# A convolution and low-rank mixer on one core: turning U first, mixing group 0 from parts, a third x buffer, group 2 mixed a round earlier

## The chip, the core and the metric

The kernel runs on one core of a Trainium2 chip. The core has a matrix engine (TensorE, PE in the profile; PEld is its weight load), VectorE (DVE), ScalarE (ACT), GpSimd (POOL) and SyncE (SP, which here only issues transfers), and sixteen DMA engines that all queues share. PE writes to PSUM; DVE and ACT carry results from PSUM to SBUF. The metric is the device time of one execution in microseconds, lower is better; the time quoted for a kernel is the median of its runs.

## The reference

All inputs are float32: `x` (8, 4224, 192), `weight` (8, 7), `U` (4224, 32), `V` (32, 4224), `w_ch1` (192, 768), `w_ch2` (768, 192).

```python
w = softmax(weight)                                  # per head, over 7 taps
out = einsum('hk,bskhg->bshg', w, x_unf)             # causal convolution along the sequence, 8 heads of 24 channels
x = out.reshape(B, S, D)
xt = x.transpose(0, 2, 1)
h = xt @ U @ V                                       # mixes along the sequence, rank 32
u = x + h.transpose(0, 2, 1)
ch = np.maximum(u @ w_ch1, 0.0) @ w_ch2
return (u + ch).astype(np.float32)
```

## The kernel before, in words

A sequence of 4224 positions is 33 tiles of 128 rows, so the eight batches have 264 tiles. Instructions are issued in an order written out by hand; each engine runs its own in that order and waits on semaphores.

*Per batch.* `load_x` (L87) brings x from HBM on POOL's queue and casts it to bfloat16. The convolution (`conv_two`, L355 to L377) is a product of x with a banded 128 x 128 matrix per head (`band_sb`), two heads at a time; DVE and ACT evict it to `y_sb`. In batches 0 and 1 a second band matrix takes in the rows of the tile before; later batches get these rows from `conv_halo` and `put_halo`. `low_rank` (L414) multiplies the 33 tiles with U and adds them up in four parts, one for each 32 partitions; `fold` (L434) adds the four with one float32 product against `fold_sb`, and gives `tt_sb`, which lies twice, in partitions 0 to 31 and 64 to 95.

*Per group of 8 tiles* (33 groups). `mix_quad` (L443) multiplies V with `tt_sb` for four tiles, and two DVE additions (L467) add `y_sb` and write `u_sb`. `u_sb` must then be turned to channels by rows: group 1 by PE (`turn`, L526 and L537), all later ones by a transposing DMA on SP's queue (`turn_by_dma`, L542); group 0 is made in turned form at once by `straight` (y turned by PE, L488) and `straight_mix` (V mixed onto it in the same PSUM bank, L504, evicted at L513 and L515). `h1_chunk` (L560) forms six chunks with W1, each evicted with a relu by ACT (L570; chunks 0, 2, 4, 5) or DVE (L572; chunks 1, 3). `w2_step` (L582) multiplies with W2; after 24 of its 48 steps per group DVE adds u (L593), and SP stores the result (L600).

*Rounds.* Round g runs `h1_chunk` for group g, then the second half of the W2 steps of group g-1 and the first half of group g's, in eight pieces. Beside the pieces stand other steps, by a table (`beside`): the turn and the mixing of group g+2, and the convolution, low rank and fold of batches to come. A step with place END comes after the last piece. In rounds 0 to 2:

- round 0: h1 of group 0; quads of group 1 and 0; W2 steps; the PE turn of group 1
- round 1: a quad of group 2, h1 of group 1, the other quad of group 2; the turn of group 2 by DMA after piece 2; the convolution of batch 1; at the end its low rank, and between its steps the two quads of group 3 and the turn of group 3 by DMA
- round 2: a quad of group 4, h1 of group 2, the other quad; `build_halo_band` (L315) at piece 0

*Start.* U arrives with 33 rows of 4096 numbers and is turned by PE in four lots of eight float32 transposes (`turn_U`, L192), evicted by `evict_U`; two lots come ahead of batch 0's convolution, two inside it. x of batch 0 comes in five loads (`blocks_0`). `load_others` brings V, W1, W2 and batch 1.

*Pools that matter.* All PSUM is one pool of four two-bank tiles (`big`), taken in rotation by every step: a tile is free when its last user has been evicted. `xs`, the x buffers, has two; the loads of batch 2 and later wait for the convolution of the batch two before.

Of the kernel before, what the change touches and what calls it, by code (L numbers as in the profile page):

```python
# [15 lines left out]
def kernel(  # L16
# [39 lines left out]
    dram = ctx.enter_context(tc.tile_pool(name="dram", bufs=2, space=bass.MemoryType.DRAM))  # L56
    xs = ctx.enter_context(tc.tile_pool(name="xs", bufs=2))
    hxs = ctx.enter_context(tc.tile_pool(name="hxs", bufs=2))
# [17 lines left out]
    x_tiles, hx_tiles = {}, {}  # L76
    blocks_0 = [(0, 8), (8, 16), (16, 24), (24, 30), (30, NT)]
    assert blocks_0[0][1] >= GT
    blocks = [(s, min(s + CB, NT)) for s in range(0, NT, CB)]
# [23 lines left out]
    w_sb = cst.tile([H, KC], F32, name="w_sb")  # L103
    nc.sync.dma_start(out=w_sb[:], in_=weight[:])

    U_rows = cst.tile([NT, P * R], F32, name="U_rows")
    U_dram = moe_U[:].rearrange("(j p) r -> j (p r)", p=P)
    nc.scalar.dma_start(out=U_rows[:, 0 : HB * R], in_=U_dram[:, 0 : HB * R])
    nc.sync.dma_start(out=U_rows[:, HB * R :], in_=U_dram[:, HB * R :])
    new_x(0)  # L110
# [52 lines left out]
    at_tap = cst.tile([KC, KC, NQ, Q], BF16, name="at_tap")  # L163
    load_x(0, *blocks_0[1])
    for s in blocks_0[2:]:
        load_x(0, *s)
    band_sb = cst.tile([P, H, 2, P], BF16, name="band_sb")
    nc.vector.memset(band_sb[:].rearrange("p h w c -> p (h w c)").bitcast(U32), 0)
    halo_band = cst.tile([HJ * HP, H, P], BF16, name="halo_band")
    V_sb = cst.tile([P, S], BF16, name="V_sb")  # L170
    W1_sb = cst.tile([P, KB, M4], BF16, name="W1_sb")
    W2_sb = cst.tile([P, MC, D], BF16, name="W2_sb")
# [9 lines left out]
    ident_32 = cst.tile([NT, NT], F32, name="ident_32")  # L182
    nc.vector.tensor_copy(out=ident_32[:], in_=ident[0:NT, 0:NT])
    U_sb = cst.tile([P, R, NT], BF16, name="U_sb")
# [14 lines left out]
    def evict_U(n, ups):  # L199
        src = ups[:, 0, 0 : UR * NT]  # L200
        dst = U_sb[:, n * UR : (n + 1) * UR, :].rearrange("p r j -> p (r j)")
        if n % 2 == 0:
            nc.scalar.activation(out=dst, in_=src, func=ACT.Copy)  # L203
        else:
            nc.vector.tensor_copy(out=dst, in_=src)

    def keep_busy(n):
# [21 lines left out]
        scale=0.0,  # L229
    )  # L230
    nc.vector.tensor_scalar_add(s_sb[:], s_sb[:], 1e-9)
    rs_sb = cst.tile([H, 1], F32, name="rs_sb")
# [4 lines left out]
    )  # L237
    for q in range(1, NQ):
        nc.vector.tensor_copy(out=in_band[q * Q : (q + 1) * Q], in_=in_band[0:Q])
    keep_busy(2)  # L240
    taps_ps = big(BF16)
    nc.tensor.transpose(out=taps_ps[0:KC, 0, 0:H], in_=tapsT[:], identity=ident[0:H, 0:H])
    taps = cst.tile([KC, H], BF16, name="taps")
    nc.vector.tensor_copy(out=taps[:], in_=taps_ps[0:KC, 0, 0:H])
    keep_busy(1)


    cps = big()
    for c in range(KC):
# [6 lines left out]
        )  # L256
    U_turned = [turn_U(0), turn_U(1)]
    local = cst.tile([P, H, NA * KC], BF16, name="local")
# [22 lines left out]
    for n, ups in enumerate(U_turned):  # L281
        evict_U(n, ups)
    nc.vector.memset(V_sb[:, 0 : S // 2].bitcast(U32), 0)

# [52 lines left out]
    def load_others():  # L337
        first = GT * P
        nc.gpsimd.dma_start(out=V_sb[0:R, 0:first], in_=moe_V[:, 0:first])
        for h in range(2):  # L340
            nc.gpsimd.dma_start(
                out=W1_sb[h * HB : (h + 1) * HB],
                in_=moe_w_ch1[:].rearrange("(k r) m -> r k m", r=HB),
            )
        nc.gpsimd.dma_start(out=V_sb[0:R, first:], in_=moe_V[:, first:])
        nc.gpsimd.dma_start(out=V_sb[HB : HB + R, :], in_=moe_V[:])
        nc.gpsimd.dma_start(out=W2_sb[:], in_=moe_w_ch2[:].rearrange("(m p) d -> p m d", p=P))
        new_x(1)
        for s in blocks:
            load_x(1, *s)  # L350
# [27 lines left out]

    hy_tiles = {}

# [33 lines left out]
    def low_rank(b, j0, j1):  # L414
        y_sb = y_tiles[b]
        n = P // R
        if b not in tps_tiles:
            tps_tiles[b] = big()
        tps = tps_tiles[b]
        for j in range(j0, j1):  # L420
            q = j % n
            nc.tensor.matmul(  # L422
                out=tps[q * R : (q + 1) * R, 0, 0:D],
                lhsT=U_sb[:, :, j],
                rhs=y_sb[:, j, :],
                start=(j < n),
                stop=(j >= NT - n),
            )
        if j1 == NT:
            tf = tfs.tile([P, D], F32, name="tf_sb")  # L430
            nc.vector.tensor_copy(out=tf[:], in_=tps[:, 0, 0:D])  # L431
            tt_tiles[b] = tf
# [64 lines left out]
    def straight_mix(g, yts):  # L497

        b, j0 = divmod(g * GT, NT)
        V_by = V_sb[:].rearrange("p (j c) -> p j c", c=P)  # L500
        ut = uts.tile([P, KB, HT, P], BF16, name="uT_sb")
        for k in range(KB):
            for t in range(2):
                nc.tensor.matmul(  # L504
                    out=yts[k][t * HB : (t + 1) * HB, :].rearrange("p (i c) -> p i c", c=P),
                    lhsT=tt_tiles[b][0:HB, k * HB : (k + 1) * HB],
                    rhs=V_by[0:HB, j0 + t : j0 + GT : 2, :],
                    start=False,
                    stop=True,
                )  # L510
            dst = ut[:, k].rearrange("p i c -> p (i c)")
            if k == 1:
                nc.vector.tensor_copy(out=dst, in_=yts[k])  # L513
            else:
                nc.scalar.activation(out=dst, in_=yts[k], func=ACT.Copy)  # L515
        ut_tiles[g] = ut
# [89 lines left out]
    for n, (s0, s1) in enumerate(blocks_0):  # L606
        for hh in range(0, H, 2):
            conv_two(0, s0, s1, hh, hh // 2 % 2, 2)
        if n < 2:
            evict_U(2 + n, turn_U(2 + n))  # L610
        if n == 0:
            nc.vector.memset(V_sb[:, S // 2 :].bitcast(U32), 0)
            load_others()
            halo_masks()
    for s0, s1 in blocks_0:
        low_rank(0, s0, s1)
    yts = [straight(0, k) for k in range(KB - 1)]
    fold(0)
    yts.append(straight(0, KB - 1))
    straight_mix(0, yts)  # L620
    new_x(2)
# [13 lines left out]
    def add(g, piece, step):  # L635
        beside[g].append((piece, step))

    add(0, 5, lambda: turn(1))
    add(1, 2, lambda: turn_by_dma(AHEAD))
    for g in range(2, NG - AHEAD):  # L640
        add(g, 2, lambda g=g: turn_by_dma(g + AHEAD))

    for n, u in enumerate(units):
        add(1, (n + 1) * 5 // len(units), lambda n=n, u=u: conv_two(1, *u, n % 3 != 2, 2))
    add(1, NP - 1, lambda: low_rank(1, 0, NT))
    add(1, END, lambda: mix_quad(3, 0))
    add(1, END, lambda: fold(1))
    add(1, END, lambda: mix_quad(3, QT))
    add(1, END, lambda: turn_by_dma(3))
    add(2, 0, build_halo_band)  # L650
    for nb in range(2, B):
# [17 lines left out]
    for g in range(NG + 1):  # L669

        if g == 0:
            quads = [], [(1, 0), (1, QT), (0, 0), (0, QT)]
        elif g == 1:
            quads = [(2, 0)], [(2, QT)]
        elif g + AHEAD < NG:
            quads = [(g + AHEAD, 0)], [(g + AHEAD, QT)]
        else:
            quads = [], []
# [47 lines left out]
```

## Time and profile before

| | us |
|---|---|
| median of three runs | 345.8 (342.67, 345.8, 346.07) |
| profiled execution | 343.05 |
| its span | 341.2 |
| PE busy | 329.2 |
| DVE busy | 224.2 |
| ACT busy | 193.1 |

The span is the stretch from the first to the last instruction; 1.85 us of the profiled execution lie outside it. Busy times of the engines overlap, since they work side by side. The groups of instructions that recur below, with the mean time of one:

| line | what | count | mean ns |
|---|---|---|---|
| L560 | W1 product, 64 x 512 | 1188 | 376 |
| L582 | W2 product, 192 columns | 1584 | 246 |
| L570 | relu on ACT, 128 x 1024 | 132 | 1022 |
| L572 | relu on DVE, 128 x 1024 | 66 | 1218 |
| L467 | addition on DVE, 128 x 384 | 128 | 549 |
| L593 | output addition on DVE | 67 | 946 |

Matmuls overlap, so a mean time is longer than the distance from one to the next: the chain of waits has 36 of L560 in 3.9 to 4.06 us. In the chain of waits a line reads: start in us from the span's start, duration in us, engine or transfer, tile and source line, and how many instructions are merged. In the timeline a bracket gives the idle time before the instruction and what ended it. Of the 31 turns by DMA the median time from issue to landing is 4.0 us.

### The profile page before, as it was taken

The numbers are of one execution on the slowest core, as the hardware profiler recorded it, in microseconds if no ns is written. First come the engines' busy times: TensorE is split into PE (matmuls) and PEld (weight loads), VectorE is DVE, ScalarE is ACT, GpSimd is POOL, SyncE is SP. The second block draws the span as 40 slices with busy tenths as digits, with TensorE's granted clock in tenths as the row PEclk, the third lists the DMA queues.
The fourth block names the chain that finished last, engine by engine and source line by source line (L and its number), as shares of the span: only waits on it lengthen the run. The fifth ranks groups of instructions, "written<-read, shape, count | busy, mean of one in ns | idle before, by whom it ended". The sixth has DMA issues, their size and how long they took to land.

```text
span 341.2 us, 8411 instructions
## 1 busy us (share of the span) xinstructions
PE 329.2 (96%) x3663; PEld 232.8 (68%) x3663; DVE 224.2 (66%) x323; ACT 193.1 (57%) x220; POOL 43.7 (13%) x70
## 2 busy tenths in 40 slices
PE   4998998999999999999999999999999999999995
PEld 2856666666677777766676777776677767777775
DVE  6758574667666556776766656667677767777553
ACT  5456647676555756666555745685565434444550
POOL 7680050050005000140005000000000000000000
PEclk9999999999999999999999999999999999999999
DMA  8999999999955996599947997535247444464424
GB/s 127 198 197 193 180 151 164 221 186 192 231 162 119 200 210 174 99 207 167 255 140 134 205 200 158 170 102 161 95 138 149 140 140 138 140 140 140 139 95 138
DMA packets 122965, 55.40 MB, mean 162 GB/s; under 512 B 88266, under 2 KB 122730, under 8 KB 122794
## 3 DMA queue, kind: packets, MB, share of 16 engines
q1 hardware_dynamic: 83988, 39.31, 48.4%
q0 software_dynamic: 38896, 15.29, 37.8%
q8 instruction: 28, 0.46, 0.5%
q10 hardware_dynamic: 44, 0.27, 0.3%
q14 instruction: 9, 0.07, 0.1%
HBM read 31.56 MB, written 26.39 MB: 170 GB/s over the span
## 4 chain that ended last, share of the span: by engine, by line
PE 90%; DMA 6%; ACT 1%; DVE 1%; issue 0%; POOLq 0%
PE big L582 38%; PE big L560 36%; PE big L365 8%; PE big L455 4%; DMA uT_sb<-u_sb 4%; DMA x_sb<-in_x_dram 2%; PE big L422 2%; PE big L436 1%; PE big L192 1%; ACT rl_sb L570 1%; PE big L388 1%; DVE o_sb L593 0%; DVE u_sb L467 0%; ACT uT_sb L537 0%; PE big L526 0%
## 5 line engine op out<-in xcount | busy, mean ns | idle before, releaser
L570 ACT ACTIVATE rl_sb<-big 128x1024 bf16<-128x1024 f32 x132 | 131.6, 1022 | 92.0 <-DVE o_sb L593 35.6
L582 PE MATMUL big<-W_sb,rl_sb 128*128 128x192 bf16 x1584 | 148.6, 246 | 0.0
L582 PEld LDWEIGHTS <-rl_sb 128*128 128x128 bf16 x1584 | 130.4, 98 | 14.4 <-issue 5.7
L560 PE MATMUL big<-uT_sb,W_sb 64*128 64x512 bf16 x1188 | 133.8, 376 | 2.0 <-DMA uT_sb<-u_sb 1.4
L593 DVE TENSOR_TENSOR o_sb<-big,u_sb 128x768 f32<-128x768 f32 (+1 forms) x67 | 63.4, 946 | 84.3 <-PE big L582 84.3
L560 PEld LDWEIGHTS <-W_sb 64*128 64x128 bf16 x1188 | 58.2, 94 | 64.8 <-DVE u_sb L467 6.8
L572 DVE TENSOR_SCALAR rl_sb<-big 128x1024 bf16<-128x1024 f32 x66 | 78.1, 1218 | 4.0 <-PE big L560 3.6
L375 ACT ACTIVATE y_sb<-big 128x1008 bf16<-128x1008 f32 (+4 forms) x64 | 48.8, 769 | 36.5 <-PE big L365 35.8
L467 DVE TENSOR_TENSOR u_sb<-y_sb,big 128x384 bf16<-128x384 bf16 x128 | 64.8, 549 | 5.5 <-PE big L455 5.4
L87 POOL DMA_DIRECT2D x_sb<-in_x_dram x19 | 21.8, 1153 | 139.4 <-PE big L365 138.2
L365 PE MATMUL big<-x_sb,band_sb 128*128 128x504 bf16 (+4 forms) x208 | 38.0, 302 | 1.0 <-DMA x_sb<-in_x_dram 0.9
L455 PE MATMUL big<-tt_sb,V_sb 64*128 64x192 bf16 x264 | 22.1, 245 | 1.0 <-ACT rl_sb L570 0.6
L365 PEld LDWEIGHTS <-band_sb 128*128 128x128 bf16 x208 | 18.3, 101 | 3.0 <-ACT U_sb L203 1.0
L455 PEld LDWEIGHTS <-V_sb 64*128 64x128 bf16 x264 | 10.5, 94 | 13.6 <-issue 6.4
L97 POOL DMA_DIRECT2D hx_sb<-in_x_dram x24 | 13.7, 577 | 0.0
L377 DVE CAST y_sb<-big 128x384 bf16<-128x384 f32 (+4 forms) x12 | 6.8, 570 | 4.5 <-PE big L365 4.1
L440 DVE CAST tt_sb<-big 128x192 bf16<-128x192 f32 x8 | 2.9, 357 | 9.4 <-PE big L436 9.4
L422 PE MATMUL big<-y_sb,U_sb 128*32 128x192 bf16 x264 | 7.7, 252 | 0.0
L422 PEld LDWEIGHTS <-U_sb 128*32 128x32 bf16 x264 | 6.2, 139 | 1.2 <-issue 1.1
L397 ACT ACTIVATE hy_sb<-big 48x384 bf16<-48x384 f32 x12 | 5.2, 478 | 2.6 <-PE big L388 2.6
L436 PE MATMUL big<-tf_sb,fold_sb 128*128 128x192 f32 x16 | 4.3, 348 | 0.2 <-DVE tf_sb L431 0.2
L209 PE MATMUL big<-ident 128*128 128x512 bf16 x3 | 1.6, 617 | 2.8 <-POOL ident L129 2.8
(68 smaller groups left out, 53.2 us busy)
## 6 DMA issues: line engine op xcount, KB each, us to landing
out_dram<-o_sb SPq DMA_DIRECT2D x65, 384.0 KB, 3.3
x_sb<-in_x_dram POOLq DMA_DIRECT2D x7, 1008.0 KB, 13.4
x_sb<-in_x_dram POOLq DMA_DIRECT2D x7, 576.0 KB, 17.3
x_sb<-in_x_dram POOLq DMA_DIRECT2D x3, 384.0 KB, 7.5
W_sb<-in_moe_w_ch_dram POOLq DMA_DIRECT2D x3, 288.0 KB, 7.6
hx_sb<-in_x_dram POOLq DMA_DIRECT2D x24, 36.0 KB, 16.9
uT_sb<-u_sb SPq DMA_TRANSPOSE x31, 4.0
hy_dr<-hy_sb SPq DMA_DIRECT2D x6, 72.0 KB
```

The lines of the kernel that those rows point to most:

```text
L87: nc.gpsimd.dma_start(out=x_tiles[b][:, 1 + s0 : 1 + s1, :], in_=x[b, s0 * P : s1 * P, :].rearrange("(j p) d -> p j d", p=P),)
L97: nc.gpsimd.dma_start(out=hx[:, s, :], in_=bass.AP(src.tensor, src.offset, [[D, HP], [HS * P * D, HJ], [1, D]]),)
L365: nc.tensor.matmul(out=cps[:, q, 0:n], lhsT=band_sb[:, hh + q, w, :], rhs=x_sb[:, 1 + s0 - w : 1 + s1 - w, hc], start=(w == 0), stop=(w == ...
L375: nc.scalar.activation(out=dst, in_=src, func=ACT.Copy)
L422: nc.tensor.matmul(out=tps[q * R : (q + 1) * R, 0, 0:D], lhsT=U_sb[:, :, j], rhs=y_sb[:, j, :], start=(j < n), stop=(j >= NT - n),)
L455: nc.tensor.matmul(out=ups[:, t, i * D : (i + 1) * D], lhsT=V_sb[rows, j * P : (j + 1) * P], rhs=tt_tiles[b][rows, :], start=True, stop=True,)
L467: nc.vector.tensor_tensor(out=dst, in0=y_tiles[b][:, j : j + 2, :].rearrange("p t (k r) -> p t k r", r=HB), in1=add, op=ALU.add,)
L560: nc.tensor.matmul(out=h1[:, q, :], lhsT=W1_sb[rows, k, m * P : (m + 1) * P], rhs=ut[rows, k, :, :], start=(k == 0), stop=(k == KB - 1),)
L570: nc.scalar.activation(out=rl, in_=src, func=ACT.Relu)
L572: nc.vector.tensor_scalar_max(out=rl, in0=src, scalar1=0.0)
L582: nc.tensor.matmul(out=ch[:, t % w, 0:D], lhsT=rl_tiles[g][:, m, t, :], rhs=W2_sb[:, m, :], start=(m == 0), stop=(m == MC - 1),)
L593: nc.vector.tensor_tensor(out=o_sb[:, 0:w, :].rearrange("p t (k r) -> p t k r", r=HB), in0=ch[:, 0:w, 0:D].rearrange("p t (k r) -> p t k r ...
```

## The change

- *U turned first.* All four lots of `turn_U` come ahead of batch 0's convolution, and all are evicted by ACT. U arrives in two loads on SP's queue (before: one on ACT's, one on SP's); the weights move from SP's queue to ACT's.
- *Batch 0's blocks.* Four blocks, to tiles 12, 22, 29 and 33, in place of five, to 8, 16, 24, 30 and 33.
- *Order on DVE at the start.* `ident_32` and the copies of `in_band` move behind the softmax and the taps.
- *Group 0 mixed from parts.* `low_rank` writes the four unfolded parts in bfloat16 (`part_sb`). V's first 1024 columns lie four times one below the other, so that `straight_mix` contracts all 128 partitions, parts and copies of V, without the fold. The fold of batch 0 comes after it, and the first `straight` ahead of `low_rank`.
- *Loads.* V's first columns come in one load that fills all partitions, W1 in four loads (halves of its columns) in place of two, the rest of V in two. The memset of V covers only the rest.
- *Three buffers for x.*
- *Group 2 in round 0.* Its two quads and its turn by DMA come at the end of round 0; the quads of group 3 take the place of group 2's in round 1, and the turn of group 3 comes after piece 2 there. `build_halo_band` moves from round 2, piece 0, to the end of round 1.

```diff
-    xs = ctx.enter_context(tc.tile_pool(name="xs", bufs=2))
+    xs = ctx.enter_context(tc.tile_pool(name="xs", bufs=3))
...
-    blocks_0 = [(0, 8), (8, 16), (16, 24), (24, 30), (30, NT)]
-    assert blocks_0[0][1] >= GT
+    blocks_0 = [(0, 12), (12, 22), (22, 29), (29, NT)]
...
-    nc.sync.dma_start(out=w_sb[:], in_=weight[:])
+    nc.scalar.dma_start(out=w_sb[:], in_=weight[:])
...
-    nc.scalar.dma_start(out=U_rows[:, 0 : HB * R], in_=U_dram[:, 0 : HB * R])
-    nc.sync.dma_start(out=U_rows[:, HB * R :], in_=U_dram[:, HB * R :])
+    for h in range(2):
+        half = slice(h * HB * R, (h + 1) * HB * R)
+        nc.sync.dma_start(out=U_rows[:, half], in_=U_dram[:, half])
...
-        if n % 2 == 0:
-            nc.scalar.activation(out=dst, in_=src, func=ACT.Copy)
-        else:
-            nc.vector.tensor_copy(out=dst, in_=src)
+        nc.scalar.activation(out=dst, in_=src, func=ACT.Copy)
...
-    for q in range(1, NQ):
-        nc.vector.tensor_copy(out=in_band[q * Q : (q + 1) * Q], in_=in_band[0:Q])
     keep_busy(2)
     taps_ps = big(BF16)
     nc.tensor.transpose(out=taps_ps[0:KC, 0, 0:H], in_=tapsT[:], identity=ident[0:H, 0:H])
     taps = cst.tile([KC, H], BF16, name="taps")
     nc.vector.tensor_copy(out=taps[:], in_=taps_ps[0:KC, 0, 0:H])
+    for q in range(1, NQ):
+        nc.vector.tensor_copy(out=in_band[q * Q : (q + 1) * Q], in_=in_band[0:Q])
     keep_busy(1)
...
-    U_turned = [turn_U(0), turn_U(1)]
+    U_turned = [turn_U(n) for n in range(R // UR)]
...
-    nc.vector.memset(V_sb[:, 0 : S // 2].bitcast(U32), 0)
+    nc.vector.memset(V_sb[:, V1 : (V1 + S) // 2].bitcast(U32), 0)
...
-        first = GT * P
-        nc.gpsimd.dma_start(out=V_sb[0:R, 0:first], in_=moe_V[:, 0:first])
+        nc.gpsimd.dma_start(
+            out=V_sb[:, 0:V1],
+            in_=bass.AP(moe_V.tensor, moe_V.offset, [[0, P // R], [S, R], [1, V1]]),
+        )
+        W1_by = moe_w_ch1[:].rearrange("(k r) m -> r k m", r=HB)
+        for m in (slice(0, M4 // 2), slice(M4 // 2, M4)):
+            for h in range(2):
+                nc.gpsimd.dma_start(out=W1_sb[h * HB : (h + 1) * HB, :, m], in_=W1_by[:, :, m])
         for h in range(2):
-            nc.gpsimd.dma_start(
-                out=W1_sb[h * HB : (h + 1) * HB],
-                in_=moe_w_ch1[:].rearrange("(k r) m -> r k m", r=HB),
-            )
-        nc.gpsimd.dma_start(out=V_sb[0:R, first:], in_=moe_V[:, first:])
-        nc.gpsimd.dma_start(out=V_sb[HB : HB + R, :], in_=moe_V[:])
+            nc.gpsimd.dma_start(out=V_sb[h * HB : h * HB + R, V1:], in_=moe_V[:, V1:])
...
         if j1 == NT:
+            if b == 0:
+                part = tts.tile([P, D], BF16, name="part_sb")
+                nc.vector.tensor_copy(out=part[:], in_=tps[:, 0, 0:D])
+                parts[b] = part
...
-                    lhsT=tt_tiles[b][0:HB, k * HB : (k + 1) * HB],
-                    rhs=V_by[0:HB, j0 + t : j0 + GT : 2, :],
+                    lhsT=parts[b][:, k * HB : (k + 1) * HB],
+                    rhs=V_by[:, j0 + t : j0 + GT : 2, :],
...
-        if n < 2:
-            evict_U(2 + n, turn_U(2 + n))
         if n == 0:
-            nc.vector.memset(V_sb[:, S // 2 :].bitcast(U32), 0)
+            nc.vector.memset(V_sb[:, (V1 + S) // 2 :].bitcast(U32), 0)
             load_others()
             halo_masks()
+    yts = [straight(0, 0)]
     for s0, s1 in blocks_0:
         low_rank(0, s0, s1)
-    yts = [straight(0, k) for k in range(KB - 1)]
+    yts += [straight(0, k) for k in range(1, KB)]
+    straight_mix(0, yts)
     fold(0)
-    yts.append(straight(0, KB - 1))
-    straight_mix(0, yts)
...
-    add(1, 2, lambda: turn_by_dma(AHEAD))
-    for g in range(2, NG - AHEAD):
-        add(g, 2, lambda g=g: turn_by_dma(g + AHEAD))
+    for i0 in (0, QT):
+        add(0, END, lambda i0=i0: mix_quad(AHEAD, i0))
+    for g in range(NG - AHEAD):
+        add(g, 2 if g else END, lambda g=g: turn_by_dma(g + AHEAD))
...
-    add(1, END, lambda: mix_quad(3, 0))
     add(1, END, lambda: fold(1))
-    add(1, END, lambda: mix_quad(3, QT))
-    add(1, END, lambda: turn_by_dma(3))
-    add(2, 0, build_halo_band)
+    add(1, END, build_halo_band)
...
-        elif g == 1:
-            quads = [(2, 0)], [(2, QT)]
```

## The prediction

> **What bounds the kernel now.** I read the table of stretches first, to see where TensorE (PE) has room at all.
>
> ```profile
> core 0: us, PE busy (x) PEld busy (x) DVE busy (x) ACT busy (x) POOL busy (x), PEclk, DMA share, GB/s
> 0.00:10.00 10.00, 5.30 (x36) 3.77 (x37) 6.57 (x22) 4.62 (x8) 6.89 (x18) 1.00 0.96 136
> 10.00:20.00 10.00, 9.96 (x140) 8.75 (x138) 6.16 (x14) 4.63 (x11) 8.04 (x16) 1.00 1.34 202
> 20.00:30.00 10.00, 8.96 (x101) 5.63 (x100) 7.26 (x12) 5.57 (x7) 4.98 (x7) 1.00 1.59 192
> 50.00:60.00 10.00, 8.65 (x92) 6.44 (x88) 5.43 (x9) 7.16 (x9) 0.00 (x0) 1.00 1.44 176
> 100.00:120.00 20.00, 20.00 (x218) 13.67 (x216) 13.79 (x19) 13.47 (x16) 4.75 (x6) 1.00 0.95 161
> ```
>
> From 60 us on PE is full, on work that the change leaves alone; its instruction order there is the same. So the change is worth what it moves the start of round 3's first product, now at 60.19. Next the chain of waits, in order of time.
>
> ```profile
> 1.33 7.22 DMA x_sb<-in_x_dram
> 8.68 2.72 PE big L365 x16
> 11.40 1.00 PE big L192 x8
> 12.40 1.43 PE big L365 x16
> 13.83 1.00 PE big L192 x8
> 14.83 2.00 PE big L365 x24
> ...
> 21.82 3.52 PE big L560 x30
> ...
> 48.17 11.98 DMA uT_sb<-u_sb
> 60.19 4.06 PE big L560 x36
> ```
>
> The first x block lands at 1.33 + 7.22 = 8.55. The convolution then runs to 18.28 with two U turns (L192, 2.0 us) inside it; round 0 begins at 21.82. Group 3's turn by DMA, issued at 48.17, holds PE back from 58.77 to 60.19: 1.42 us. Last, VectorE (DVE) and GpSimd (POOL) in the timeline.
>
> ```profile
> 26.24 3.81 DVE L467 TENSOR_TENSOR u_sb<-y_sb,big 128x384 bf16<-128x384 bf16 x8 [0.29 <-PE big L455]
> 30.49 0.96 DVE L593 TENSOR_TENSOR o_sb<-big,u_sb 128x768 f32<-128x768 f32 x1 [0.45 <-PE big L582]
> 31.37 1.01 DVE L467 TENSOR_TENSOR u_sb<-y_sb,big 128x384 bf16<-128x384 bf16 x2
> 32.51 2.52 DVE L572 TENSOR_SCALAR rl_sb<-big 128x1024 bf16<-128x1024 f32 x2
> 44.35 2.49 POOL L87 DMA_DIRECT2D x_sb<-in_x_dram  x2 [19.10 <-PE big L365]
> ```
>
> DVE has almost no gap where round 0 passes into round 1, which is where the change puts more of its work. POOL waits 19.10 us for a free x buffer.
>
> **The start: U turned ahead.** Two turns (16 transposes, 2.0 us) leave the convolution and join the other 16 in front of it. The taps copy no longer stands behind three in_band copies (0.88 us on DVE), so the turns begin between 5.1 and 5.79, where they begin now; I take 5.45. At 1.96/16 = 0.1225 us each, 32 end at 9.4. Their four evictions, all on ScalarE (ACT), 0.39 each, lie beside that, and each PSUM buffer is evicted before its next user needs it. Both U halves now sit on SP's queue and the weights on ACT's: the order of issue changes, not the bytes, and no wait for either is in the trace, so nothing. If U came late, each us would push the turns a us, with 0.4 us of cover up to x's landing.
>
> x: blocks of 8, 8, 8, 6 and 3 tiles land now at 8.55, 10.9, 12.9, 14.6 and 15.3 (POOL's issue times plus 7.2, 7.5, 8.6, 9.3 and 9.2). The new blocks end at tiles 12, 22, 29 and 33: halfway between two landings and 0.15 for a longer issue gives 9.85; then 12.4, 14.3 and 15.4.
>
> So the convolution starts at 9.85, 1.2 later than now, but without the turns in it. Its pace: the first 16 matmuls of 192 columns took 2.72 us, the next 1.43, with the granted clock given as 1.00 throughout. So PE was slow until 11.4, for 2.7 us of convolution, though 16 transposes had run from 5.79 to 7.75. Going by that row, 2.7 us of the new first block (16 matmuls of 288 columns: 1.9 us quick, 3.8 slow) run slowly: it ends at 9.85 + 2.7 + 0.6 = 13.2. The others take 1.6, 1.15 and 0.95 us quick: 14.8, 15.95, 16.9, all behind x's landings. Now: 18.28. (The Trainium skill, "TensorE: Matmul & The Clock Gate", Part 1, has a half-rate clock that opens after about 3.4 us of sustained activity; 4 us of unbroken transposes should open it before the convolution. By that rule x's landings bound the blocks, it ends at 16.45, and the sum is 0.4 us better. The row speaks against it, the transposes being an odd small shape.)
>
> From there to round 0, now 18.28 to 21.82 = 3.54 us. The change takes the fold out of the path: straight(0) 0.3, low_rank 0.9, two more straights 0.57, six mixing matmuls 0.83, the fold behind them 0.55: 3.15 us. The added part copy on DVE (0.36, the row of tf_sb) lies under the two straights; uncovered it would cost 0.36. The mixing contracts 128 rows for 64 with the same columns; wide and narrow straights run side by side in the same way, so no difference. Round 0 begins at 20.05: **1.8 us earlier**.
>
> W1 must be there. It now lands at 17.1 and 18.4; the first part of V grows from 64 to 256 KB, W1 keeps its bytes in four loads for two. At 288 KB in 1.3 us that adds about 0.9 us, and shorter rows perhaps 0.6: its first half, enough for three chunks, at 18.2, the rest at 20 where 22 is needed. Covered by 1.9 us. x of batch 1 moves 1.3 us later, to 29.5 and 32.5, and is wanted from about 35: covered. V's first load skips the 1.8 us wait for a memset; the two memsets shrink from 1056 to 800 words (0.94 to 0.7 us each) in DVE's gaps.
>
> **Rounds 0 to 2**, in the old frame. Group 2 is mixed at the end of round 0, and group 3's first quad follows ahead of round 1's products. DVE is then in series: o_sb 30.49 to 31.45, six adds at 0.505 to 34.48, relu of chunk 1 (1.22) to 35.70, chunk 3 to 36.92. Big PSUM tiles are four in rotation: the quad of group 3 takes o_sb's tile (31.45), chunks 1, 2 and 3 take those of the three quads (32.46, 33.47, 34.48), and the first output matmuls take chunk 3's: 36.97 where it was 35.16. That is **+1.8 us** of PE waiting; bounds 0 (adds hidden) and 3.0 (six adds whole). Behind it: SP's transposes and the first out store stay in order, the turn of group 2 issuing at 33.5 for 36.32.
>
> Taken away: the 1.42 wait, since group 3's turn issues at about 38 and is wanted at 60; 0.5 of halo band and its DVE wait in round 2 (52.17 to 53.31 now), which fits into the wait for tt_sb at the end of round 1, where 0.15 more is saved. Sum +1.8 - 1.42 - 0.5 - 0.15: **0.3 us earlier**.
>
> **Three x buffers.** Loads of batch 3 queue right behind batch 2 (25 rather than 44.35), of batch 4 when batch 1's convolution ends (41 rather than 68.77); behind that wait POOL has only loads of later batches. PE waited for x only once, at the start, so this gains nothing. It costs if the turns by DMA suffer. Group 2's issues at 33.5 - 1.8 = 31.7 and is wanted at 47.2 (47.37 less the 0.15; the two 1.8 cancel): 15.5 us, against 11.98 for the worst now. Covered by 3.5. (The skill's "DMA: Bandwidth & Descriptors", Queues, rings and completion order, lets each DMA engine take turns between queues packet by packet, so a backlog would at most halve a turn's share: 8 us from the median 4.0, an estimate. The 11.98 here is worse than that.)
>
> Sum: 1.8 + 0.3 = 2.1, and 343.05 becomes 340.95 for the profiled execution (span 341.2, 1.85 around it). The median of the runs is 345.8, 2.75 above, at the upper end of 342.67 to 346.07; one trace cannot say if what makes that spread is in the start. I carry half of it: 342.4.
>
> **Rivals.** (a) *The clock opens late.* If PE stays slow for twice 2.7 us, to 15.25, the first block ends at 13.7, the second at 16.1 and the convolution at 18.15: the start gains 0.5, the whole 0.8; on my basis 343.7. For it: the slow stretch above; against: quick after 2.7 us now. (b) *The DVE queue doesn't bind*: adds drain while PE mixes, +1.8 becomes 0, and the whole gains 3.9: 340.6. For: it needs only an earlier o_sb or freer tiles; against: DVE's rows are back to back there. (c) *Slower: group 2's turn is late.* With three batches of x queued it might land like the x load issued at 20.5 to 22, which took 20.6 us: 31.7 + 20.6 = 52.3 for 47.2, +5.1, a loss of 3.0: 347.4. It costs from 15.5 us on and turns the sign from 17.6. Against: 11.98 with a backlog of the same kind. (d) *The gain at the start isn't one*, x landing setting the end: already in the blocks, whose last lands at 15.4; only a 1.5 us later landing would cost.
>
> **Numbers.** Forecast 0.57, (a) 0.18, (b) 0.15, (c) 0.10. 1% of 345.8 is 3.5 us, about what a measurement tells from no change, so the line is at 342.3: the forecast falls on both sides (0.27 faster, 0.30 same), (a) 0.03 and 0.15, (b) 0.13 and 0.02, (c) 0.04 same, 0.06 slower. Faster 0.43, same 0.51, slower 0.06. Range: low end (b) with less of the spread, 339.5; high end 346.0, the forecast and (a) with the whole spread (343.7, 345.0) and a part of (c).
>
> **What would show it.** Convolution from 9.85 without L192 inside it, ending by 16.9; round 0 from 20; no wait for uT_sb in round 3; in round 1 waits of L560 for u_sb adds; POOL without its 19.10 us. Wrong if round 0 starts after 21, if round 2 waits for its turn, or if the time from round 0 to round 3 isn't 38 us (38.37 now).

## The result, and where the time went

The changed kernel takes 346.7 us, the median of 20 runs from 345.11 to 348.74; the kernel before, in 20 runs beside them, 345.5. The ratio is 1.0055 with a 95% interval of 1.0031 to 1.0078: slower, by less than 1%. The profiled execution took 345.11 us (343.05 before).

The first lines of its page and the shares of its chain of waits:

```profile
span 343.4 us, 8379 instructions
PE 329.3 (96%) x3647; PEld 232.8 (68%) x3647; DVE 222.4 (65%) x320; ACT 193.6 (56%) x220; POOL 44.6 (13%) x71
PE 83%; DMA 11%; DVE 3%; POOL 1%; ACT 1%; issue 0%
```

PE does the same 329 us of work in a span 2.2 us longer: the time is in waiting. (The profile is of the fastest of the 20 runs.) The chain of waits of the changed kernel, in order of time (start, duration, what), shows for what:

```profile
7.29 13.03 DMA V_sb<-in_moe_V_dram
20.36 0.84 PE big L507 x6
21.72 3.43 PE big L563 x30
...
48.54 3.88 PE big L563 x36
...
58.97 3.88 PE big L563 x36
...
68.34 3.89 PE big L563 x36
...
75.18 25.56 DMA uT_sb<-u_sb x2
100.78 4.06 PE big L563 x36
```

L563 is the first product of a round (L560 before). Round 0 begins at 21.7 where the forecast had 20.05 and the kernel before 21.82: the start brought 0.1 in place of 1.8. Round 3 begins at 58.97 for 60.19, round 4 at 68.34 for 69.73: up to there the kernel is 1.4 us ahead. Then the chain passes through two turns by DMA, issued at 75.18 and 84.40, and round 7 begins at 100.78 where it began at 98.78, in the chain of the kernel before:

```profile
98.78 3.89 PE big L560 x36
```

The 2.0 us stay to the end. PE's timeline has the two waits (the bracket is the idle time and what ended it):

```profile
89.21 4.06 PE L563 MATMUL big<-uT_sb,W_sb 64*128 64x512 bf16 x36 [0.70 <-DMA uT_sb<-u_sb]
100.78 4.06 PE L563 MATMUL big<-uT_sb,W_sb 64*128 64x512 bf16 x36 [2.52 <-DMA uT_sb<-u_sb]
```

They are rounds 6 and 7. The turn that round 7 waits for is in SP's timeline, changed kernel and kernel before (the second number is how long SP took to issue it):

```profile
84.40 8.67 SPq L545 DMA_TRANSPOSE uT_sb<-u_sb  x1
84.49 5.33 SPq L542 DMA_TRANSPOSE uT_sb<-u_sb  x1
```

Its last packet ended at 100.2 and it was reported landed at 100.7; before, its last packet had ended at 92.3. From issue to last packet that is 15.8 us for 7.8. Round 7 could have begun at 98.26 (100.78 less the wait of 2.52), so the turn had 13.9 us of cover. The list of DMA issues from 50 to 110 us, changed kernel, gives size and median us from issue to landing:

```profile
x_sb<-in_x_dram POOLq DMA_DIRECT2D x3, 1008.0 KB, 25.2
x_sb<-in_x_dram POOLq DMA_DIRECT2D x3, 576.0 KB, 31.7
...
uT_sb<-u_sb SPq DMA_TRANSPOSE x6, 14.2
```

The same list of the kernel before:

```profile
x_sb<-in_x_dram POOLq DMA_DIRECT2D x2, 1008.0 KB, 13.3
x_sb<-in_x_dram POOLq DMA_DIRECT2D x2, 576.0 KB, 17.5
...
uT_sb<-u_sb SPq DMA_TRANSPOSE x7, 8.4
```

Three batches of x land in that stretch for two, and each load takes about twice as long. The row of the turns rests on little: the trace has the landing of one of the six (issued at 95.39, 14.2 us) and, before, of two of the seven (48.17, 12.0 us; 95.08, 4.8 us). The turn issued near 95 is the same one in both. In the table of stretches, changed kernel (the last columns are PEclk, the DMA share as printed, and GB/s), the queues never empty:

```profile
80.00:90.00 10.00, 9.30 (x121) 6.62 (x119) 6.18 (x10) 4.89 (x5) 1.68 (x3) 1.00 1.41 190
90.00:100.00 10.00, 8.26 (x92) 5.88 (x86) 6.46 (x9) 5.29 (x6) 0.00 (x0) 1.00 1.37 189
```

Before, batch 4 is through by then and the share falls to half:

```profile
80.00:90.00 10.00, 10.00 (x129) 7.08 (x127) 6.19 (x11) 6.01 (x6) 0.00 (x0) 1.00 1.47 204
90.00:100.00 10.00, 10.00 (x110) 6.85 (x108) 7.25 (x11) 5.77 (x7) 0.00 (x0) 1.00 0.68 189
```

Why the loads come so is in the timeline of POOL, changed kernel:

```profile
52.73 2.48 POOL L86 DMA_DIRECT2D x_sb<-in_x_dram  x2
...
67.76 2.49 POOL L86 DMA_DIRECT2D x_sb<-in_x_dram  x2 [1.24 <-PE big L364]
...
108.37 2.49 POOL L86 DMA_DIRECT2D x_sb<-in_x_dram  x2 [20.52 <-PE big L364]
```

These are the loads of batches 4, 5 and 6. Before, batch 4 was issued at 68.77 and batch 5 only at 106.59. With the third buffer two batches are loaded back to back across the turns of groups 6 and 7.

The start, in PE's timeline of the changed kernel:

```profile
5.71 3.73 PE L191 MATMUL big<-ident,U_rows 33*128 33x33 f32 x32 [0.80 <-DMA U_rows<-in_moe_U_dram]
9.94 7.27 PE L364 MATMUL big<-x_sb,band_sb 128*128 128x288 bf16 x56 [0.50 <-ACT U_sb L201]
17.41 0.50 PE L364 MATMUL big<-x_sb,band_sb 128*128 128x96 bf16 x8 [0.20 <-ACT y_sb L374]
...
20.36 0.84 PE L507 MATMUL big<-V_sb,part_sb 128*64 128x512 bf16 x6 [0.65 <-DMA V_sb<-in_moe_V_dram]
21.65 4.13 PE L563 MATMUL big<-uT_sb,W_sb 64*128 64x512 bf16 x36
```

The turns wait 0.80 us for U and still end at 9.44; the convolution starts at 9.94 and ends 0.95 us later than forecast. About 0.5 of that comes from the half pace of its matmuls, which lasts until 13.6, for 3.7 us where the forecast had 2.7; the mixing then waits 0.65 us for V, whose load took 13.03 us. Behind V stood W1: the two loads of its first half landed at 20.83 and 21.68, so that round 0, whose first chunk needs both, could not have begun much before 21.7 even if V had been there.

Below, "the clock opens" means the moment at which the distance between convolution matmuls halves (in the kernel before from 160 to 82 ns for 192 columns). The profile's clock column reads 1.00 on both sides of it.

### The profile page after: what moved, and what is told of

Read it like the earlier page. It is cut to its first block, busy times and chain, and to the rows that moved or that the text cites. A ratio compares the mean times of both kernels' runs of the same rounds, so it can differ in the third digit from the quotient of the medians.

```text
span 343.4 us, 8379 instructions
## 1 busy us (share of the span) xinstructions
PE 329.3 (96%) x3647; PEld 232.8 (68%) x3647; DVE 222.4 (65%) x320; ACT 193.6 (56%) x220; POOL 44.6 (13%) x71
## 4 chain that ended last, share of the span: by engine, by line
PE 83%; DMA 11%; DVE 3%; POOL 1%; ACT 1%; issue 0%
PE big L585 36%; PE big L563 34%; DMA uT_sb<-u_sb 7%; PE big L364 6%; DMA V_sb<-in_moe_V_dram 4%; PE big L458 3%; PE big L421 1%; PE big L439 1%; DVE u_sb L470 1%; POOL x_sb L86 1%; DVE o_sb L596 1%; DVE rl_sb L575 1%; PE big L387 1%; ACT rl_sb L573 1%; DVE band_sb L167 0%; PE big L507 0%
## 5 line engine op out<-in xcount | busy, mean ns | idle before, releaser
L563 PE MATMUL big<-uT_sb,W_sb 64*128 64x512 bf16 x1188 | 134.3, 376 | 3.6 <-DMA uT_sb<-u_sb 3.2
L563 PEld LDWEIGHTS <-W_sb 64*128 64x128 bf16 x1188 | 58.6, 94 | 66.3 <-DVE u_sb L470 7.6
L374 ACT ACTIVATE y_sb<-big 128x576 bf16<-128x576 f32 (+4 forms) x62 | 48.5, 788 | 35.5 <-PE big L364 34.9
L364 PE MATMUL big<-x_sb,band_sb 128*128 128x288 bf16 (+4 forms) x192 | 38.0, 316 | 0.8 <-ACT U_sb L201 0.5
L364 PEld LDWEIGHTS <-band_sb 128*128 128x128 bf16 x192 | 17.6, 102 | 4.0 <-ACT U_sb L201 0.6
L96 POOL DMA_DIRECT2D hx_sb<-in_x_dram x24 | 13.6, 576 | 48.0 <-DMA x_sb<-in_x_dram 33.8
L376 DVE CAST y_sb<-big 128x576 bf16<-128x576 f32 (+4 forms) x10 | 6.3, 645 | 8.2 <-PE big L364 8.1
```

What stands on the lines that cost most here:

```text
L96: nc.gpsimd.dma_start(out=hx[:, s, :], in_=bass.AP(src.tensor, src.offset, [[D, HP], [HS * P * D, HJ], [1, D]]),)
L364: nc.tensor.matmul(out=cps[:, q, 0:n], lhsT=band_sb[:, hh + q, w, :], rhs=x_sb[:, 1 + s0 - w : 1 + s1 - w, hc], start=(w == 0), stop=(w == ...
L563: nc.tensor.matmul(out=h1[:, q, :], lhsT=W1_sb[rows, k, m * P : (m + 1) * P], rhs=ut[rows, k, :, :], start=(k == 0), stop=(k == KB - 1),)
```

## The experiments

Two theories were tested first: that the third buffer costs the time, by way of the turns by DMA, and that the start costs it, by V's load and a clock that opens later. Each was taken out alone, then both.

**a_two_x.** The changed kernel with two x buffers.

```diff
-    xs = ctx.enter_context(tc.tile_pool(name="xs", bufs=3))
+    xs = ctx.enter_context(tc.tile_pool(name="xs", bufs=2))
```

> The changed kernel with two x buffers again. Theory 1 (the third buffer queues the loads of batches 4 and 5 back to back, the turns by DMA of groups 6 and 7 land late and PE waits 0.7 and 2.5 us): no wait for uT_sb in rounds 6 and 7, profiled execution near 345.1 - 3.2 = 341.9, ratio to the kernel before about 0.993 to 0.997. Theory 2 (the waits come from the backlog that V's first load leaves on a few DMA engines, whatever the buffers): waits of 2 us or more remain, profiled execution near 345, ratio about 1.005.

Measured: 342.29 us (341.81 to 342.76, 12 runs), ratio to before 0.9934 [0.9907, 0.9961]. PE waits for no turn by DMA in any round. Its list of DMA issues from 50 to 110 us:

```profile
x_sb<-in_x_dram POOLq DMA_DIRECT2D x2, 1008.0 KB, 12.9
x_sb<-in_x_dram POOLq DMA_DIRECT2D x2, 576.0 KB, 16.8
...
uT_sb<-u_sb SPq DMA_TRANSPOSE x6, 3.2
```

Two batches again, and the one turn whose landing the trace has, issued at 94.94, takes 3.2 us for 14.2. So the third buffer turned a gain into a loss: 346.7 less 342.29 is 4.4 us between the medians. The waits that it adds are 3.2 us in the profile. (Between the two profiles lie 2.35 us, but the one of the changed kernel is of its fastest run and this one of the slowest of twelve.)

**b_three_x.** The kernel before with three x buffers, and nothing else.

```diff
-    xs = ctx.enter_context(tc.tile_pool(name="xs", bufs=2))
+    xs = ctx.enter_context(tc.tile_pool(name="xs", bufs=3))
```

> The kernel before with a third x buffer and nothing else. Theory 1: turns by DMA late in rounds 4 to 8, waits of PE for uT_sb of 2 to 4 us in sum, profiled execution near 346, ratio 1.006 to 1.012. Theory 2: V loads as before, so no new wait, ratio 1.000.

Measured: 345.5 us (344.19 to 346.29, 12 runs), 1.0009 [0.998, 1.0038]: no difference, a miss. The mechanism is there: PE waits 3.0 us for turns in three rounds, 1.96 of it in round 7, for a turn that took 16.11 us; the kernel before waits 1.42, in round 3 alone. Yet the median does not move. before_again_1 and 2 below show why it could: the times of the kernel before lie in two heaps, near 343 and near 346. With three buffers the lower heap is gone; the profiled execution, whose clock opened early, at 11.9, took 345.0. That a later start is absorbed by the wait for the turns, so that only the lower heap pays, fits; it is argued and not shown.

**c_v_split** and **d_two_x_v_split.** V's first columns in four loads of 32 partitions in place of one load that reads its source four times; in c with three x buffers, in d with two.

```diff
-        nc.gpsimd.dma_start(
-            out=V_sb[:, 0:V1],
-            in_=bass.AP(moe_V.tensor, moe_V.offset, [[0, P // R], [S, R], [1, V1]]),
-        )
+        for q in range(P // R):
+            nc.gpsimd.dma_start(out=V_sb[q * R : (q + 1) * R, 0:V1], in_=moe_V[:, 0:V1])
```

> The changed kernel with V's first columns loaded by four loads of 32 partitions in place of one load whose source repeats four times. If the one load ran on 4 of the 16 DMA engines (128 packets of 173 ns took 5.5 us), V now lands near 17 in place of 20.3, the 0.65 us wait of the group 0 mixing goes and round 0 begins near 21.0. Theory 1: the waits in rounds 6 and 7 stay at 2 to 3.5 us, profiled execution near 344.5. Theory 2: they go, near 341.5.

> Both: two x buffers and V in four loads. Theory 1: no wait for uT_sb, no wait for V, profiled execution near 341.2, ratio 0.990 to 0.996, the fastest of the four. Theory 2: the same as V split alone.

Measured: c 345.44 (343.56 to 347.05, 12 runs), 1.002 [0.9988, 1.0052]; d 341.54 (340.57 to 342.05, 9 runs), 0.9904 [0.9873, 0.9934]. In both the wait for V is gone. Round 0 does not begin near 21.0 in them, as was expected of c, but at 21.94 and 21.95: their clock opened at 15.4 and 15.1. In c the wait for turns has not gone: 0.7 us in round 6, and in round 7 the weight load waits 1.9 us for a turn that landed at 100.27, while the first product, at 100.32, is put down to an addition to `u_sb` that ended at the same moment. Against a_two_x, d is 0.75 us faster, about the 0.5 us that a_two_x waited for V. So V's load costs somewhat under 1 us and the third buffer the larger part, 3.9 us between c and d.

In the trace of the changed kernel the 128 packets of V's one load took 173 ns each, 22.1 us of engine time, between 13.73 and 19.28: 22.1 / 5.55 is 4.0 engines at work. This is what the Trainium skill gives in "DMA: Bandwidth & Descriptors", section "Why a DMA increments its semaphore by 16 and not by 1": a transfer runs on the largest number of engines, up to 16, that divides the outermost dimension of both sides, here 4 (the copies) and 128 (the partitions).

**before_again_1** and **before_again_2.** The kernel before, for two more profiles, to see what makes its two heaps: of its 20 runs beside the changed kernel's seven lie below 344 and thirteen above 345.2.

> The kernel before, unchanged, for another profile: its 52 times so far fall into two heaps, near 343 and near 346, and the one profile is of the lower heap. If the time is near 346: either PE waits longer for a turn by DMA (theory A: group 3's turn, 1.42 us in the profile so far, 4 us here), or the clock opens later or closes again (theory B: no longer wait, but matmuls at half pace for some 3 us more).

> The same again, for the heap that the first look missed. Theory A: a wait for uT_sb that is 3 us longer in the upper heap. Theory B: a longer slow stretch of PE.

Measured: 345.77 and 342.87, one of each heap. PE's timeline of the first:

```profile
9.04 2.72 PE L365 MATMUL big<-x_sb,band_sb 128*128 128x192 bf16 x16 [1.03 <-DMA x_sb<-in_x_dram]
...
12.71 2.74 PE L365 MATMUL big<-x_sb,band_sb 128*128 128x192 bf16 x16
...
16.41 4.88 PE L365 MATMUL big<-x_sb,band_sb 128*128 128x192 bf16 x48
21.21 0.96 PE L422 MATMUL big<-y_sb,U_sb 128*32 128x192 bf16 x33
```

The same view of the profile that the prediction was made from:

```profile
12.33 1.49 PE L365 MATMUL big<-x_sb,band_sb 128*128 128x192 bf16 x16
...
14.76 3.52 PE L365 MATMUL big<-x_sb,band_sb 128*128 128x192 bf16 x48
18.21 0.96 PE L422 MATMUL big<-y_sb,U_sb 128*32 128x192 bf16 x33
```

The second block of 16 takes 2.74 us or 1.49. In the upper heap the clock opens at 19.74, in the lower at 11.3 to 11.5; round 0 begins at 24.82 or 21.8, and that 3.0 us is the distance between the heaps. So the prediction's profile was of the lower heap, while the median of the kernel before lies in the upper one. The profiles of the changed kernel and of those made from it with U turned ahead have the clock open between 13.6 and 17.7. The times of a_two_x, d, e and g lie in one heap each, 1.0 to 2.3 us wide. A longer wait for group 3's turn, the other explanation of the heaps, is out: it is 1.28 us in the upper heap's profile and 1.42 to 1.45 in the lower one's.

**e_dense_between.** d with six matmuls of 512 columns, into a PSUM bank that nobody reads, two ahead of the first lot of U turns and one behind each lot, to open the clock before the convolution.

```diff
+        for _ in range(2 if n == 0 else 0):
+            nc.tensor.matmul(out=ups[:, 1, :], lhsT=ident[:], rhs=ident_4, start=True, stop=True)
...
+        nc.tensor.matmul(out=ups[:, 1, :], lhsT=ident[:], rhs=ident_4, start=True, stop=True)
```

> Two x buffers and V in four loads, and beside that six 512-column matmuls of the identity that serve nothing, two ahead of the U turns and one behind each lot. Theory 1 (float32 transposes of 33 columns don't open the clock, so the convolution runs slowly for 4 to 5 us): with dense matmuls among the turns the clock opens before 13 us in place of 15.1, and round 0 begins near 21 in place of 22.0, or as now if the opening comes by chance of phase. Theory 2 (the slow stretch has another cause, as x arriving): no earlier start, and up to 0.9 us lost to the added matmuls.

Measured: 342.83 (342.2 to 343.96, 10 runs), 0.9943 [0.991, 0.9976]; slower than d by 1.3 us. In its profile, which is of the slowest of the ten runs, the clock opened later, at 17.7, and round 0 began at 24.17. A miss: six dense matmuls spread among the turns did not open it.

**i_u_inside.** d with two of the four U lots back inside the convolution, as before the change.

```diff
-    U_turned = [turn_U(n) for n in range(R // UR)]
+    U_turned = [turn_U(0), turn_U(1)]
...
+        if n < 2:
+            evict_U(2 + n, turn_U(2 + n))
```

> Two x buffers and V in four loads, but two lots of U turned inside the convolution again, as before the change. If U turns inside the convolution keep the clock shut (openings of the kernel before: 11.3 to 11.5 or 19.7), two heaps come back about 3 us apart, near 341 and 344, the clock opening near 12 or near 19 to 20; median above 342.5. If the two heaps of the kernel before have another cause, one heap, near 342.

Measured: 343.23 (342.41 to 346.46, 12 runs), 0.9954 [0.992, 0.9987]: nine runs up to 343.45, three from 344.47 to 346.46. Turning U ahead is worth 1.7 us between the medians of d and i (the kernel before stood at 345.84 and 345.9 beside them). The three high runs look like the heap of before, but they are few and spread, and the profile (clock open at 15.2, round 0 at 23.51) is of the lower group: that turns inside the convolution cause the two heaps is not settled.

**f_group2_alone.** The kernel before with only the mixing and turn of group 2 in round 0 and `build_halo_band` in round 1.

```diff
-    add(1, 2, lambda: turn_by_dma(AHEAD))
-    for g in range(2, NG - AHEAD):
-        add(g, 2, lambda g=g: turn_by_dma(g + AHEAD))
+    for i0 in (0, QT):
+        add(0, END, lambda i0=i0: mix_quad(AHEAD, i0))
+    for g in range(NG - AHEAD):
+        add(g, 2 if g else END, lambda g=g: turn_by_dma(g + AHEAD))
...
-    add(2, 0, build_halo_band)
+    add(1, END, build_halo_band)
```

> The kernel before with only the mixing and turning of group 2 moved to round 0, group 3 a place earlier and build_halo_band at the end of round 1. From the traces, round 0 to round 3 should take 37.2 us in place of 38.4: 1.2 us less on the profile of the lower heap, ratio 0.996. If the upper heap of the kernel before comes from waiting for group 3's turn (theory A), this removes it: times in one heap near 342, ratio near 0.990.

Measured: 344.85 (341.65 to 345.07, 12 runs), 0.9991 [0.9957, 1.0026]. Its profile has round 0 to round 3 in 37.18 us (24.67 to 61.85) where the kernel before takes 38.37 (38.23 in before_again_1): 1.1 to 1.2 less. Its times lie in two heaps too, 341.65 to 342.93 and 344.54 to 345.07, the upper about 1 us below the upper one of before, two of the lower three likewise; nine of twelve fell in the upper, so the medians hide the gain.

**after_again_1** and **after_again_2.** The changed kernel as it is, for two more profiles.

> The changed kernel, unchanged, for another profile: its 20 times reach from 345.1 to 348.7 and its one profile is of the fastest. If the clock's opening is not what spreads them (it opened at 13.6 there), a time of 346.5 or more shows longer waits for the turns of groups 5 to 8, 4 to 6 us in sum, or a clock that closes again during one of them.

> The same again: waits for uT_sb of 3 to 6 us in sum, and the clock opening between 13 and 17 us, never near 19.7.

Measured: 347.49 and 346.51, with waits for turns of 3.3 us (two rounds, longest 2.5) and 3.5 us (three, longest 2.2), and the clock opening at 16.3 and 16.4. The loss is no accident of one profile. In the first something came on top. Its table of stretches (busy time of PE, PEld, DVE, ACT and POOL with counts, then PEclk, DMA share and GB/s):

```profile
95.00:98.00 3.00, 3.00 (x38) 2.90 (x36) 1.19 (x2) 1.64 (x3) 0.00 (x0) 1.00 1.41 145
98.50:101.40 2.90, 0.51 (x7) 0.12 (x5) 1.88 (x3) 0.00 (x0) 0.00 (x0) 1.00 1.37 192
101.50:105.00 3.50, 3.50 (x18) 1.35 (x20) 0.70 (x1) 1.02 (x1) 0.00 (x0) 0.52 1.37 255
```

After a wait of 2.5 us, with PE busy for 0.51 of 2.9 us, the granted clock is 0.52, and in 3.5 us PE does 18 matmuls. The clock was closed for 3.41 us, and the product of round 7 took 5.75 us for its usual 4.06: 1.7 us more. The Trainium skill, "TensorE: Matmul & The Clock Gate", Part 1, gives a window of 3413 ns, which this duration agrees with; it has an idle window of about 3.4 us close the clock, and here a wait of 2.5 was enough. In the other two profiles of this kernel, waits of 2.5 and 2.2 us left the clock open.

**h_four_x.** Four x buffers (with V in four loads): more of the suspect.

```diff
-    xs = ctx.enter_context(tc.tile_pool(name="xs", bufs=3))
+    xs = ctx.enter_context(tc.tile_pool(name="xs", bufs=4))
```

> Four x buffers and V in four loads: the dose raised. If loads that run ahead crowd out the turns by DMA, the load of batch 6 also comes early (some 90 us in place of 108) and more turns are late, in rounds 5 to 10: waits for uT_sb of 4 us or more against 2.4 with three buffers, median 346 or more. If the number of buffers as such is without effect beyond the third, 345.4 as with three.

Measured: 350.84 (348.83 to 352.59, 4 runs), 1.0144 [1.0081, 1.0207]. Three batches now load back to back (the load of batch 6 is issued at 86.25, for 108.37 with three buffers). The waits, as line and what it waited for, us in total, times, longest:

```profile
PE big L561 <- DMA uT_sb<-u_sb: 9.9, 7, 2.4
```

With two, three and four buffers (d, c, h, all with V split) the medians are 341.54, 345.44 and 350.84.

**k_three_x_held.** Three buffers, but the loads of batches 3 to 7 start no earlier than with two: ahead of them POOL copies 24 numbers that the convolution of the batch two before writes last.

```diff
+                nc.gpsimd.tensor_copy(
+                    out=held[HB : HB + 1, :], in_=y_tiles[nb - 2][HB : HB + 1, NT - 1, D - GS :]
+                ),
                 new_x(nb),
                 [load_x(nb, *s) for s in blocks],
                 load_halo(nb),
```

> Three x buffers and V in four loads, but ahead of the loads of batch 3 and later GpSimd copies 24 numbers of the convolution's result of the batch two before, so that the loads start no earlier than with two buffers. If the time of the loads is the cause, and not the buffer's place or count: no wait for uT_sb, median near 341.5 as with two buffers. If something else of the third buffer is, near 345.4.

Measured: 342.45 (340.97 to 343.14, 10 runs), 0.992 [0.9889, 0.9951]. POOL's timeline:

```profile
46.36 0.20 POOL L665 COPY held<-y_sb 1x24 bf16<-1x24 bf16 x1 [17.49 <-ACT y_sb L373]
47.38 2.49 POOL L86 DMA_DIRECT2D x_sb<-in_x_dram  x2 [0.82 <-PE big L584]
...
68.59 0.20 POOL L665 COPY held<-y_sb 1x24 bf16<-1x24 bf16 x1 [15.80 <-ACT y_sb L373]
69.16 2.48 POOL L86 DMA_DIRECT2D x_sb<-in_x_dram  x2 [0.36 <-PE big L457]
```

The loads of batches 3 and 4 go at 47.38 and 69.16, as with two buffers, and PE waits for no turn by DMA. There are three buffers as in c; besides a copy of 24 numbers only the time of the loads differs, and it brings 3.0 us (the kernel before beside c and k: 345.84 and 345.86). This settles the cause: loads that start early, not the third buffer as such. 0.9 us to d remain; in the profiles k's clock opened at 16.0 for 15.1 and its round 0 began 0.5 us later, the rest is open. How the loads hold up a turn, by its packets or already by its issue, which took SP 8.67 us for 5.33, was not taken apart.

**g_blocks_5** and **n_u_two_queues.** d with the five x blocks of before, and in n also U's halves and the weights on the queues of before: a search for a better version of the start.

```diff
-    blocks_0 = [(0, 12), (12, 22), (22, 29), (29, NT)]
+    blocks_0 = [(0, 8), (8, 16), (16, 24), (24, 30), (30, NT)]
```

> Two x buffers, V in four loads, and the five x blocks of the kernel before (first block 8 tiles). The convolution no longer waits for x after the U turns, so it starts near 9.6 in place of 10.5. If the clock opens in the first stretch of some 3.4 us that convolution fills (openings seen: 13.6 to 15.4), an earlier start gains 0.5 to 1 us on average: median near 341.0 against 341.5. If the larger blocks matter (fewer evictions), 341.5 to 342.5.

> Two x buffers, V in four loads, five x blocks, and U's halves on two queues (ScalarE's and SyncE's) with the weights on SyncE's, as before the change. If both halves on one queue delay U, the wait of the turns for U (1.4 us with one queue, 0 to 0.7 before the change) falls by some 0.5 us and round 0 begins 0.2 to 0.5 earlier: median near 340.3. If the order of queues is nothing, 340.6.

Measured: g 340.62 (339.75 to 342.06, 6 runs), 0.987 [0.9828, 0.9913]; n 340.42 (340.34 to 341.36, 6 runs), 0.9869 [0.9829, 0.9908]. The two are not to be told apart. PE's timeline of g:

```profile
9.82 8.12 PE L362 MATMUL big<-x_sb,band_sb 128*128 128x192 bf16 x80
...
20.92 1.25 PE L561 MATMUL big<-uT_sb,W_sb 64*128 64x512 bf16 x10
```

The convolution starts at 9.82 without a wait for x, where d waited 0.7 us for its longer first block, and round 0 begins at 20.92. Either version is about 1.3% faster than the kernel before and 1.8% (340.62 / 346.7) faster than the changed one.

## Why the prediction was wrong

The time lies 0.7 us above the range's end and 4.3 above the forecast. By its own steps:

*Three x buffers: "this gains nothing. It costs if the turns by DMA suffer."* This is the step that failed. The cover was worked out for the turn of group 2 alone, 15.5 us against the worst turn of before, 11.98, and the forecast put nothing down. (The usual 4.0 us of a turn was the median of the ten landings that the trace has for 31 turns: five near 3.2 us and five from 4.8 to 12.0, so no turn was usual.) But the text had named batch 4's loads coming forward, from 68.77 to 41 (52.73 it became), and the price of that falls on the turns that then run beside batches 4 and 5: groups 6 and 7. The turn of group 7 has 13.9 us from its issue at 84.40 to the time at which round 7 could begin, less than the 15.5 of group 2, and it took 15.8 us to its last packet where it had taken 7.8. The text's estimate for a turn beside a backlog, 8 us, was half of that. The cost is 4.4 us between the medians, 3.2 of it seen as waits in the profile. The remaining 1.2 is not fully accounted for; the clock that closed after such a wait, 1.7 us in one of three profiles, is a part.

*Rival (c)*, a turn late because three batches of x are queued, had the mechanism and, with 347.4, nearly the time. It had the wrong place (group 2 in round 2; that turn held nobody up) and a chance of 0.10. The reason given against it, 11.98 "with a backlog of the same kind", compared one batch queued ahead with two back to back.

*The start: 1.8 us earlier.* Against the lower-heap profile it brought 0.1; round 0 after 21 was one of the text's own signs of being wrong. Conv start 9.85 was right to 0.1 (the U wait of 0.80, put at nothing, pushed the turns to an end of 9.44 for 9.4, because they ran from 5.71 for 5.45). The slow stretch, 2.7 us "by that row", was 3.7 here, and 6.0 and 5.7 in the other two profiles of this kernel: the row was one draw of two, and the worse one was hidden in the spread of the medians. The convolution ended 0.95 late. V's own landing, for which the sum had no term, cost 0.65 by running on four engines. 0.95 + 0.65 is the 1.6 us by which round 0 missed 20.05; the other steps from the convolution's end to round 0 took the 3.15 they were summed to. *"W1 must be there ... Covered by 1.9 us"* failed too: its first half, forecast at 18.2, was there at 21.68, so an earlier convolution alone would have gained nothing. With V in four loads (d) the same half landed at 17.86 and 18.61.

*Half the spread carried*, of the 2.75 between profile and median (340.95 and half of it is 342.3, not 342.4). The spread was in the start, as the text suspected, and the change closed the late heap: with two buffers it measures 3.55 us below the median of before beside it (342.29 for 345.84). Without the third buffer 342.4 would thus have been right as a sum, but by luck and not by its own steps, since the start's gain came from the heap that the profile at hand did not show.

*Rounds 0 to 2: 0.3 earlier.* Right in sign, too small: 1.2 (37.16 us from round 0 to round 3 for 38.37), and 1.1 to 1.2 in f_group2_alone. The delay of round 1's output matmuls came as 1.37 for 1.8; round 2, without the wait for its turn and the halo band, gave 2.3 for 1.92; the end of round 1 gave 0.26 for 0.15. DVE's timeline of the changed kernel has the series that the +1.8 stood for:

```profile
30.30 0.96 DVE L596 TENSOR_TENSOR o_sb<-big,u_sb 128x768 f32<-128x768 f32 x1 [0.45 <-PE big L585]
31.17 2.87 DVE L470 TENSOR_TENSOR u_sb<-y_sb,big 128x384 bf16<-128x384 bf16 x6
33.96 2.35 DVE L575 TENSOR_SCALAR rl_sb<-big 128x1024 bf16<-128x1024 f32 x2
```

It runs as foreseen without gaps, six additions and two relus, to 36.3 for 36.92; of the 0.6 us, 0.17 is the earlier round 0 of this profile. So rival (b), that DVE's queue doesn't bind, is out.

*Rival (a)*, a clock that opens late, at 15.25, came about in two of three profiles of the changed kernel (16.28 and 16.40; 13.6 in the third), and, at 19.74, in the upper heap of the kernel before, which holds most of its executions. The open question of the prediction, whether turns ahead would open the clock, has an answer: 3.73 us of unbroken transposes did not. What exactly opens it stays open.

## What to carry to other kernels

A further buffer does not only remove a wait, it moves transfers forward: list what each load will now run beside, batch by batch to the end, and price the shortest cover of every transfer on the path there, not that of the first. If the wait it removes stood on an engine with nothing else to do, as POOL's here, it may have been the pacing that kept the path free. And where the times of a kernel lie in two heaps, find out which of them the profile shows before taking durations from it.

## What was not expected of the hardware

- A start of half-pace matmuls that ends at 11.3 to 11.5 us in some executions and 19.7 in others of the same program, worth 3.0 us of 345, while the clock column reads 1.00.
- The clock can close again for 3.41 us after a wait of 2.5 us and not after another of the same length.
- A load whose source is repeated four times by a dimension of stride 0 ran on 4.0 of the 16 DMA engines; in four loads the same bytes landed at most 8.6 us after the issue of each and 9.6 after the first (c_v_split), for 13.03, and W1 behind them came 3.1 us earlier (18.6 for 21.7, d_two_x_v_split).
- The same turn by DMA took 7.8 us to its last packet where the x loads beside it ended halfway (DMA share 0.68 from 90 to 100 us) and 15.8 where they did not (1.37).
